# Attention then token mixing on one core: PSUM allocated as one tile of eight banks, and a new order of the steps

## The chip, the core and the metric

The kernel runs on one core of a Trainium2 chip. The core has a matrix engine (PE; its weight loads are listed apart as PEld), a vector engine (DVE), a scalar engine (ACT), a general engine (POOL) and a queue engine (SP) that here issues every DMA. Each engine works through its own instructions in the order in which they were written; engines wait for one another by semaphores only. The metric is device time in microseconds (us) of one execution, as the median of several.

## What is computed

Two layers, one after the other, for 8 batches of 8 heads, 576 positions and 64 columns a head:

```python
q_d = q.reshape(B, H, Sd, 4, D).mean(axis=3)      # the same for k_d, v_d; Sd = 144
out_up = np.repeat(sm_attn(q_d, k_d, v_d), 4, axis=2)      # attention over the pooled positions
scores = np.where(np.abs(pos[:, None] - pos[None, :]) < 4, scale * q @ k.T, -1e9)
out_local = softmax(scores) @ v                            # attention in a band of 7
x = (out_up + out_local)   # [batch, 576, 512], heads side by side

theta = x @ w_theta
y = w_tok_r @ (x * cos(theta)) + w_tok_i @ (x * sin(theta))
u = x + y
out = u + relu(u @ w_ch)
```

## The kernel before

Everything is unrolled. A batch goes through some thirty kinds of step, each written as a Python generator that gives one piece at a time. A string, `ORDER`, has one letter for each piece, 1,240 in all, and says in which order the pieces are recorded; `pin` then chains each engine's instructions in just that order. So the order is written out by hand, and no scheduler moves anything. A second string, `BANKS`, gives the PSUM bank for each piece that needs one.

The steps, with the letters that stand for them and the lines of their main instructions:

- `L` loads q, k and v pieces into one of 15 staging buffers `st` (SP, lines 202 and 205); `C` casts them to bfloat16 (line 218 for v, 221 for q and k; mostly POOL). `l` and `c` do the same for the weights (lines 238 and 240; POOL, 247 and 249).
- `V` and `v`: the token weights are turned on PE (line 261) and copied into `WT` by DVE (line 271), 18 pieces, the first nine for the first half of the output positions.
- `A` and `a`: q and k are turned on PE (286) and copied out by ACT (292). `d`, `e`: sums of four positions (DVE 303; POOL 320 and 321). `U`, `u`, `x`, `P`, `p`, `N`, `n`, `Q`, `q`: the pooled attention (PE 334 to 434; ACT 340, 343, 387; DVE 419, 421, 440).
- `S`, `s`, `m`: banded scores on PE (454), their exponential on ACT (466), the band's mask on DVE (474). `O`, `o`, `i`: the product with v on PE (486) and its normalization on DVE (500, 506). `T`, `t`: the result turned on PE (526) and joined with the pooled one into `xT` by DVE (538).
- `H`, `h`: theta on PE (553), and its cosine and sine by ACT (560 and 561). `G`, `g`, `Z`, `z`: the same for the last 64 positions (PE 571; ACT 578 and 579; DVE 589), with a transposing DMA on SP's queue (595). `X`, `y`: x turned on PE (605) and multiplied with cosine and sine by DVE (610) into `z`.
- `J`, `j`: the token mixing, 64 pieces of nine matmuls each (PE 630, the largest share of PE's work), and the sum `uT` with x on DVE (639). `R`, `f`, `F`: transposing DMAs for the residual (646, 657) and a small POOL copy (652).
- `K`, `b`, `E`, `r`: the channel matmul on PE (665, 671), and ReLU with the residual on DVE (678) into `osb`. `D`, `Y`: stores (691, 697).

PSUM has eight banks of 512 float32 columns. Before the change it is four tiles of two banks each, `pair0` to `pair3`:

```python
pairs = [psum.tile([P, 2, 512], FP32, name=f"pair{i}") for i in range(4)]
```

A step that needs one bank takes it with `one()`, a slice of a pair; a step that needs two takes a whole pair with `two()`. The semaphore waits are not written in the kernel: the recording layer derives them from which instruction touches which part of which tile, and it puts a wait wherever two engines touch the same place of a PSUM tile, reads against reads too.

Of the kernel before, what the change touches and what calls it, by code (L numbers as in the profile page):

```python
# [8 lines left out]
FP32 = mybir.dt.float32  # L9
# [5 lines left out]
P = 128  # L15
# [28 lines left out]
def kernel(  # L44
# [14 lines left out]
    psum = ctx.enter_context(tc.tile_pool(name="psum", bufs=1, space=bass.MemoryType.PSUM))  # L59
# [1 line left out]


    ORDER = (
        "LLkLkCCACLaCLLLALkCCLllaCLLCkLeAkaAkLLadSLeLLkSdsklkklkCcSLkmlPLCcLCCLssOmmCPUlpOCuoiLpCoLlCCOluxxAl"
        "iNncNnaCcCCcnoliTALdaAOnCaLAociLQOaqeLStdoTeTtPsltlimPCcHHplXTCLtpcchVOLHcCCoCXvVilvLlhVvXhTVtCLcyUH"
        "ucvOuyoyVGhvVixvVLxNVlnvgcSNnvSTsnVnLvVvCsZcccAVLLvzVVvVvVCXvTLvyQVValvLqmvCCtAtJaLCLVCOjLJjlmCvLoHO"
        "iOoLlJoheLTLCiJLCLAcjTLtaCiAtdCHTXCCXaLtLHCHALdheyhaChJcCyXGjJUgjyCjCSRuPZupXzCxlJyjAsLcxaLJRmCLJjLf"
        "SsOPRJLjoipCSsjCOoLANNiJCnJnmLOLCnmnaORJjcjoTRoQeLKiCTjUuLiOqtCtTCKtXbJbCHLuoiTxHACXLRjCTtLhHCaXyCtH"
        "eKhdGLhdhbJLLgJSyyjCPPsLjXLpZRyKmKxLRzpbOSsSbJoiCNsmmLNLnAJnnCALnDLCCKLLCJaCCjaObjjOQoTJDCoiKiJqTtUb"
        "ujOjDfLDuOJTCLoiDtLJdLjRoHhjAaLJtKLjiALTHbTaXtChCHCRFtGyCCdCDDRhXECeRrHLXghxeCKSysZzPXyCbyKADLaCJCpx"  # L70
        "JSmjObsoPKJjLmDipjOLoRiOoJiNjnbAaNKnnnLSsDOJACQCoLiTdRJDajqAYCCeCabTtJLTmLjOUutDLJtdoijHfLThHtTLhAjX"
        "tHaGyXKyRguHChhZXKRXSbSdyzfexbLKyJAbJssmmLOPDCCaPFjJopiCOpCjLSoCxjLOismeJNoJRjUiCOnonijDJuDNjAJnCnja"
        "TTQRAuLqLRTttTJXaOxHthtAjoiKXTLtbaHHyhHGhXELDgKdyrShZKyXRKePbbCsyzbSPCmpCxCpJNAsnNJanOSjnnComJODCijj"
        "soOQqofiJTALCYimALTaJTtCRttHaOjoOLJCXhiTJoXRijCTHyetXejhCHtGUdDhjdJgHKyuuRZyXhSjbPzyPJxsppJmSOjoiJjs"
        "JOmjOoSjoixsRiJNKTjmDnNRDnnJfnObOKooQiTJDbqtDFRKTtjHTiXtKtTjHthyHHhGEXJgbZKXhXhzbryyyjRKRJjJjJDbJJJY"
        "RDjJJjjKfKbDjjKRjbfDRRbKDbbDKbFKDDEbrDDY"
    )
    BANKS = (
        "0246024602456024624046304326432016471634562356023140624106207645076452042650645203467301746310274063"
        "6230462046204526014523064132450612543205620476204634062401640132674502645706746017623764502764704261"  # L80
        "4620462064126742567042375460753467401265405260426056452036054360725604275401402370654260520642056023"
        "2460142640367214536401376402764072406362405603267324650124152673542676730167325401"
    )


# [6 lines left out]
            made[tag, k % n] = const.tile(shape, dt, name=f"{tag}_{k % n}")  # L92
        return made[tag, k % n]

    pairs = [psum.tile([P, 2, 512], FP32, name=f"pair{i}") for i in range(4)]
    banks = iter(BANKS)

    def one(dt=FP32):
        i = int(next(banks))
        ap = pairs[i // 2][:, i % 2, :]  # L100
        return ap if dt == FP32 else ap.bitcast(dt)

    def two(dt=FP32):
        ap = pairs[int(next(banks)) // 2][:, :, :]
        return ap if dt == FP32 else ap.bitcast(dt)

    copies = dict(v=nc.vector.tensor_copy, a=nc.scalar.copy, p=nc.gpsimd.tensor_copy)
# [71 lines left out]
    def warm_up():  # L179
        while True:  # L180
            ps = one()
            nc.tensor.matmul(out=ps, lhsT=ident, rhs=warm, start=True, stop=True)
            yield
# [70 lines left out]
    def weight_turns():  # L254
        for hf in range(2):
            for j in range(9):
                ps = held["w", hf, j] = one(BF16)
                for ct in range(3):
                    for ri in ((j % 2,) if j < 8 else (0, 1)):
                        lo, n = (0, P) if j < 8 else (HALF * ri, HALF)  # L260
                        nc.tensor.transpose(
                            out=ps[lo:lo + n, OC * ct:OC * ct + OC],
                            in_=w_tm[ri][0:OC, 3 * hf + ct, P * (j // 2):P * (j // 2) + n],
                            identity=ident[0:OC, 0:OC],
                        )
                yield
# [13 lines left out]
    def turns(b):  # L280
        q_tm, k_tm, v_w = inputs[b]
        parts[b] = (rot("qT", [P, 4, S], BF16, 2), kTs[b % 2], rot("qdT", [P, 4, SD], BF16, 2), kds[b % 2])
        for i, what in TURNS:
            ps = held["turn", b, i, what] = two(BF16).rearrange("p k e -> p (k e)")
            for r in range(WR):
                nc.tensor.transpose(out=ps[:, P * r:P * r + P], in_=(k_tm if what == "k" else q_tm)[:, i, r, :, :], identity=ident)  # L286
            yield
# [41 lines left out]
    def pooled_v(b):  # L329
        v_w = inputs[b][2]  # L330
        psa = held["va", b] = one()
        psb = held["vb", b] = one()
        for c in range(4):
            nc.tensor.matmul(out=psa[KP * c:KP * c + KP, :], lhsT=PU[c], rhs=v_w[:, c, :, 0:D], start=True, stop=True)
        for c in range(4):
            nc.tensor.matmul(out=psb[KP * c:KP * c + KP, 0:2 * D], lhsT=PU[4], rhs=v_w[:, 4, c::4, 0:D], start=True, stop=True)
        yield
# [24 lines left out]
    def pooled_scores(b):  # L362
        qT, kT, qdT, kd = parts[b]

        def heads(dst, hh):
            for m in range(2):
                for par in range(2):
                    nc.tensor.matmul(out=dst(par)[64 * m:64 * m + 64], lhsT=kd[64 * par:64 * par + 64, hh, 2 * m:2 * m + 2, :],
                                     rhs=qdT[64 * par:64 * par + 64, hh, :], start=True, stop=True)

        ps = held["Sd", b, 0] = two()
        for hh in range(3):
            heads(lambda par: ps[:, par, SD * hh:SD * hh + SD], hh)
        yield
        ps = held["Sd", b, 1] = two()
        heads(lambda par: ps[:, par, 0:SD], 3)
        for h in range(H):
            r = KP * (h % 4)
            blk, par = slot(h)
            nc.tensor.matmul(out=ps[r:r + KP, h // 4, SD:2 * SD], lhsT=kd[64 * par:64 * par + 64, blk, 4, :],  # L380
                             rhs=qdT[64 * par:64 * par + 64, blk, :], start=True, stop=True)
        yield
# [390 lines left out]
```

## Time and profile before

| | |
|---|---|
| median of 3 runs | 323.38 us (323.06 to 327.02) |
| the profiled execution | 324.98 us |
| its span, first to last instruction | 323.3 us |
| mean granted clock of PE | 0.939 |
| instructions in the profile | 8,176 |
| bytes moved by DMA | 49.85 MB |

The profile names an instruction by line, engine, operation and tiles (`uT<-pair,xT`: `uT` is written, `pair` and `xT` are read). Behind the busy time of a group stands the idle time of its engine just ahead of the group's instructions, with the releasers, that is, the instructions of other engines whose end let the engine go on. A row of the waits reads: engine and line, what it waited for, the total in us, how often, and the longest. PE's clock is given as the share of full speed that was granted.

### The profile page before, as it was taken

Reading aid. Unit: us, or ns where it says so; the run is one execution under the profiler, and the core shown is the slowest. Engines: PE = TensorE matmul, PEld = TensorE weight load, DVE = VectorE, ACT = ScalarE, POOL = GpSimd, SP = SyncE. Lnnn points to the kernel's source line nnn. Section 1 sums busy time; section 2 is a strip of 40 time slices with the busy share of each in tenths; the row PEclk is TensorE's granted clock in tenths of the full one; section 3 lists DMA queues with packets and bytes.
Section 4 is the critical chain, followed back from the end, with each engine's and each line's share of the span. In section 5 each row is a group of like instructions: output and inputs, shape, how many; then the busy total and the mean of one; then the engine's idle time right before and its main releaser. Section 6 shows DMA issues by size and latency. Waiting matters only on the chain. (4 is left out here: it accounts for less than half of the span.)

```text
span 323.3 us, 8176 instructions
## 1 busy us (share of the span) xinstructions
PE 239.8 (74%) x3344; PEld 162.8 (50%) x3372; DVE 192.4 (60%) x390; ACT 137.4 (43%) x188; POOL 119.5 (37%) x215
## 2 busy tenths in 40 slices
PE   1656975759588897887689587878987888757853
PEld 1535554536356554654357445664665456434510
DVE  2775668637147778672659646667684957624251
ACT  4743656133464195215563277254925650430000
POOL 7667957442329196430704034327032100000000
PEclk9999999598699999997999989999999999997977
DMA  7999996597049998999158838471433032213263
GB/s 234 270 281 237 222 291 168 125 295 217 1 58 193 261 211 218 289 254 152 51 180 133 242 59 163 120 188 47 80 89 83 16 69 81 67 33 96 85 210 98
DMA packets 83173, 49.85 MB, mean 154 GB/s; under 512 B 68160, under 2 KB 68160, under 8 KB 83136
## 3 DMA queue, kind: packets, MB, share of 16 engines
q1 hardware_dynamic: 83136, 49.33, 61.6%
q8 instruction: 26, 0.43, 0.6%
q14 instruction: 11, 0.09, 0.1%
HBM read 34.11 MB, written 9.44 MB: 135 GB/s over the span
## 5 line engine op out<-in xcount | busy, mean ns | idle before, releaser
L630 PE MATMUL pair<-WT,z 128*128 128x288 bf16 x576 | 85.6, 300 | 13.6 <-ACT cs L561 6.1
L630 PEld LDWEIGHTS <-z 128*128 128x128 bf16 x576 | 56.9, 102 | 33.0 <-issue 14.9
L639 DVE TENSOR_TENSOR uT<-pair,xT 128x288 bf16<-128x288 f32 x64 | 28.1, 450 | 46.5 <-PE pair L630 24.6
L665 PE MATMUL pair<-wch,uT 128*128 128x512 bf16 x113 | 34.0, 410 | 11.9 <-DVE osb L678 6.7
L553 PE MATMUL pair<-wth,xT 128*128 128x512 bf16 x116 | 33.0, 404 | 12.5 <-DVE uT L639 4.5
L678 DVE SCALAR_TENSOR_TENSOR osb<-pair,ur 128x512 f32<-128x512 f32 x32 | 21.6, 685 | 24.9 <-ACT cs L561 6.4
L538 DVE TENSOR_TENSOR xT<-pair,xdT 128x464 bf16<-128x464 f32 (+1 forms) x40 | 24.5, 632 | 17.5 <-PE pair L526 5.7
L218 POOL CAST v_w<-st 128x512 bf16<-128x512 f32 x40 | 24.8, 639 | 21.1 <-DMA st<-in_v_dram 20.6
L560 ACT ACTIVATE cs<-pair,pihc 128x512 bf16<-128x512 f32 x32 | 22.1, 692 | 21.8 <-PE pair L553 8.0
L320 POOL TENSOR_TENSOR two<-qT 128x576 f32<-128x576 bf16 x14 | 16.1, 1147 | 40.7 <-ACT qT L292 40.6
L292 ACT COPY qT<-pair 128x1152 bf16<-128x1152 bf16 x16 | 17.9, 1120 | 23.3 <-PE pair L286 23.3
L652 POOL COPY ut<-uT 128x256 bf16<-128x256 bf16 x8 | 3.7, 458 | 65.4 <-DVE uT L639 62.8
L506 DVE TENSOR_TENSOR tmp<-pair,rl 128x512 bf16<-128x512 f32 x40 | 27.1, 684 | 0.7
L610 DVE TENSOR_TENSOR z<-pair,cs 128x1024 bf16<-128x1024 bf16 x32 | 21.6, 682 | 9.3 <-ACT cs L561 3.8
L292 ACT COPY kT<-pair 128x1152 bf16<-128x1152 bf16 x16 | 17.9, 1122 | 18.4 <-PE pair L286 18.4
L466 ACT ACTIVATE pm<-pair 128x1024 bf16<-128x1024 f32 (+1 forms) x24 | 20.6, 882 | 11.4 <-PE pair L454 11.3
L553 PEld LDWEIGHTS <-xT 128*128 128x128 bf16 x128 | 12.1, 102 | 24.7 <-issue 13.5
L665 PEld LDWEIGHTS <-uT 128*128 128x128 bf16 x128 | 12.5, 102 | 24.0 <-issue 14.9
L560 ACT ACT_TABLE_LOAD x8 | 10.3, 1283 | 32.9 <-PE pair L605 14.1
L221 POOL CAST k_tm<-st 128x576 bf16<-128x576 f32 x28 | 19.1, 693 | 13.3 <-DMA st<-in_k_dram 12.9
L349 POOL TENSOR_TENSOR vd<-last,own 128x256 bf16<-128x256 bf16 x16 | 9.8, 622 | 36.9 <-ACT last L343 36.9
L303 DVE TENSOR_REDUCE kd<-kT 128x290 bf16<-128x1160 bf16 x16 | 21.6, 1356 | 0.0
(77 smaller groups left out, 385.8 us busy)
## 6 DMA issues: line engine op xcount, KB each, us to landing
st<-in_v_dram SPq DMA_DIRECT2D x80, 128.0 KB, 3.9
st<-in_k_dram SPq DMA_DIRECT2D x32, 288.0 KB, 4.7
st<-in_q_dram SPq DMA_DIRECT2D x32, 288.0 KB, 5.2
out_dram<-osb SPq DMA_DIRECT2D x32, 256.0 KB, 2.4
st<-in_moe_w_tok_r_dram SPq DMA_DIRECT2D x6, 216.0 KB, 5.7
st<-in_moe_w_tok_i_dram SPq DMA_DIRECT2D x6, 216.0 KB, 6.0
st<-in_moe_w_theta_dram SPq DMA_DIRECT2D x4, 256.0 KB, 5.8
st<-in_moe_w_ch_dram SPq DMA_DIRECT2D x4, 256.0 KB, 4.6
```

The source lines that it names most:

```text
L218: copies[e](out=v_w[:, c, :, 0:D], in_=staged.pop((b, it))[:, 0:DM].rearrange("p (h d) -> p h d", d=D))
L292: copies[e](out=To[:, 2 * i:2 * i + 2, 0:S].rearrange("p a (w r) -> p a w r", r=WR), in_=held.pop(("turn", b, i, what))[:, 0:P * WR].rearr ...
L303: nc.vector.tensor_reduce(out=kd[:, hs, :, 0:PG].rearrange("p e g m -> p (e g) m"), axis=AX.X, op=ALU.add, in_=kT[:, hs, :].rearrange("p e ...
L506: nc.vector.tensor_tensor(out=tmp.rearrange("p g (j d) -> p g j d", d=D), in0=held.pop(("loc", b, c))[:, :, :, 0:D], in1=rls.pop((b, c)).u ...
L538: nc.vector.tensor_tensor(out=xT[:, :, CH * c:CH * c + cnt].rearrange("p e (m j) -> p e m j", j=4), in0=held.pop(("xT", b, c))[:, :, 0:cnt ...
L553: nc.tensor.matmul(out=th, lhsT=xT[:, dc, P * c:P * c + P], rhs=wth[:, dc, :], start=(dc == 0), stop=(dc == 3))
L560: nc.scalar.activation(out=cs[:, 0, :], in_=th, func=AF.Sin, bias=pihc, scale=1.0)
L610: nc.vector.tensor_tensor(out=z_of(b)[:, 2 * c:2 * c + 2, :], in0=held.pop(("xt", b, c)).unsqueeze(1).to_broadcast([P, 2, DM]), in1=css.po ...
L630: nc.tensor.matmul(out=ps, lhsT=z[:, j, P * dc:P * dc + P], rhs=WT[:, j, 288 * hf:288 * hf + 288], start=(j == 0), stop=(j == 8))
L639: nc.vector.tensor_tensor(out=uT[:, dc, cols], in0=held.pop(("u", b, dc, hf)), in1=xT[:, dc, cols], op=ALU.add)
L665: nc.tensor.matmul(out=ps, lhsT=uT[:, dc, P * c:P * c + P], rhs=wch[:, dc, :], start=(dc == 0), stop=(dc == 3))
L678: nc.vector.scalar_tensor_tensor(out=osb, in0=ps, scalar=0.0, in1=rest, op0=ALU.max, op1=ALU.add)
```

## The change

Two edits. PSUM becomes one tile of eight banks, `space`, of which `one()` and `two()` give the same slices as before; and `ORDER` and `BANKS` are replaced by other strings of the same length. Each letter occurs as often as before, so every instruction of the computation is there as before, with the same operands and sizes, in another order and in part in other banks. Lines from 96 on move down by one.

```diff
     ORDER = (
-        "LLkLkCCACLaCLLLALkCCLllaCLLCkLeAkaAkLLadSLeLLkSdsklkklkCcSLkmlPLCcLCCLssOmmCPUlpOCuoiLpCoLlCCOluxxAl"
-        "iNncNnaCcCCcnoliTALdaAOnCaLAociLQOaqeLStdoTeTtPsltlimPCcHHplXTCLtpcchVOLHcCCoCXvVilvLlhVvXhTVtCLcyUH"
-        "ucvOuyoyVGhvVixvVLxNVlnvgcSNnvSTsnVnLvVvCsZcccAVLLvzVVvVvVCXvTLvyQVValvLqmvCCtAtJaLCLVCOjLJjlmCvLoHO"
...
-        "RDjJJjjKfKbDjjKRjbfDRRbKDbbDKbFKDDEbrDDY"
+        "LCkkLCLLCkkLCkLALkLkkALCLLaakCAlaCLkLCLkACdlaSCCSSkcCsLLCeeLdmUussmuOmOLCLoPpPoxiCOoOCipxAaLCCLLAcio"
+        "LliCNCCaAeAnadlTNTnOlaCLdnnoCiSecQTqcLCctLPtllCtspTtCPXHTphmHtUOHuolciluOlcXLLcLGxLhyVycxvhHXNoicygL"
+        "LNnLnnCVLlSVhvVsnVSvvvZszClQCmlCVAqTVAvVLtaClCCvVOvAToaaOviTtlComAaXictHTOcyScloecstcHLiLhhJLXXTVLdc"
+        "HtGvCymJVLVCvLvHgXhZLLyVCCVJlCVvVevyvCVhvVjjvUuClvuJLLSjOOLjsJzJoiAjLLoCCXiJdxaAmJCaSCLjysCOPjLLjpPm"
...
+        "fJRDjDRDbDjbRDKKjjKbbRKbKKbfDbFDDbEDrDDY"
     )
     BANKS = (
-        "0246024602456024624046304326432016471634562356023140624106207645076452042650645203467301746310274063"
+        "0246024670246046204624306462450301546340671026042136012456012406120456210523673465135672561325026452"
...
-    pairs = [psum.tile([P, 2, 512], FP32, name=f"pair{i}") for i in range(4)]
+    space = psum.tile([P, 8, 512], FP32, name="space")
     banks = iter(BANKS)
 
     def one(dt=FP32):
         i = int(next(banks))
-        ap = pairs[i // 2][:, i % 2, :]
+        ap = space[:, i, :]
         return ap if dt == FP32 else ap.bitcast(dt)
 
     def two(dt=FP32):
-        ap = pairs[int(next(banks)) // 2][:, :, :]
+        i = int(next(banks)) // 2
+        ap = space[:, 2 * i:2 * i + 2, :]
         return ap if dt == FP32 else ap.bitcast(dt)
```

More of the change, by code (lines that the diff above doesn't have):

```diff
@@ L63 @@
     ORDER = (
-        "LLkLkCCACLaCLLLALkCCLllaCLLCkLeAkaAkLLadSLeLLkSdsklkklkCcSLkmlPLCcLCCLssOmmCPUlpOCuoiLpCoLlCCOluxxAl"
-        "iNncNnaCcCCcnoliTALdaAOnCaLAociLQOaqeLStdoTeTtPsltlimPCcHHplXTCLtpcchVOLHcCCoCXvVilvLlhVvXhTVtCLcyUH"
-        "ucvOuyoyVGhvVixvVLxNVlnvgcSNnvSTsnVnLvVvCsZcccAVLLvzVVvVvVCXvTLvyQVValvLqmvCCtAtJaLCLVCOjLJjlmCvLoHO"
-        "iOoLlJoheLTLCiJLCLAcjTLtaCiAtdCHTXCCXaLtLHCHALdheyhaChJcCyXGjJUgjyCjCSRuPZupXzCxlJyjAsLcxaLJRmCLJjLf"
-        "SsOPRJLjoipCSsjCOoLANNiJCnJnmLOLCnmnaORJjcjoTRoQeLKiCTjUuLiOqtCtTCKtXbJbCHLuoiTxHACXLRjCTtLhHCaXyCtH"
@@ L69 @@
[L69 to L73, printed above, removed]
@@ L74 @@
-        "soOQqofiJTALCYimALTaJTtCRttHaOjoOLJCXhiTJoXRijCTHyetXejhCHtGUdDhjdJgHKyuuRZyXhSjbPzyPJxsppJmSOjoiJjs"
-        "JOmjOoSjoixsRiJNKTjmDnNRDnnJfnObOKooQiTJDbqtDFRKTtjHTiXtKtTjHthyHHhGEXJgbZKXhXhzbryyyjRKRJjJjJDbJJJY"
-        "RDjJJjjKfKbDjjKRjbfDRRbKDbbDKbFKDDEbrDDY"
+        "LCkkLCLLCkkLCkLALkLkkALCLLaakCAlaCLkLCLkACdlaSCCSSkcCsLLCeeLdmUussmuOmOLCLoPpPoxiCOoOCipxAaLCCLLAcio"
+        "LliCNCCaAeAnadlTNTnOlaCLdnnoCiSecQTqcLCctLPtllCtspTtCPXHTphmHtUOHuolciluOlcXLLcLGxLhyVycxvhHXNoicygL"
@@ new lines @@
+        "LNnLnnCVLlSVhvVsnVSvvvZszClQCmlCVAqTVAvVLtaClCCvVOvAToaaOviTtlComAaXictHTOcyScloecstcHLiLhhJLXXTVLdc"
+        "HtGvCymJVLVCvLvHgXhZLLyVCCVJlCVvVevyvCVhvVjjvUuClvuJLLSjOOLjsJzJoiAjLLoCCXiJdxaAmJCaSCLjysCOPjLLjpPm"
+        "xCpLcolJTiNAjCNnRCJnRRaACOnnoLQjlJiaqjtCcTTJOSCtjLtoURXJfijTHXstmuTHXtuedxHhJLcGLRLHyLhLdhgChJyLyCjc"
+        "RjOoCeiSSJsjZsmKOCPpoLLmCPLbKiAbpxNNLCfnAnnnaXKaKQObyOTqCCzLLCDLLoitTtCJCLoijCCJHThTCJjteAaLLbjUOoCJ"
+        "juALtiRuLCJLXaRdXCdHTxhtDAJjHahyLCHyCGCLCLhLFLCeKCjPPXCDCgXKbRLpJyKZbpjySSCxUEsbNsJmrSunnDOumCLzsAaK"
@@ new lines @@
+        "AjJLoRLbijNnmOoOaTfJnRoiATRQLjiJCCqTOaDOYtKtooCXeLiCHitLTAbhRHtKCTjDaDtCxXyhXLCdHxGHJbeLJhgdyjJjyLhS"
+        "jPPJppdDRKAsjLLZKLzRNXbCLamSbyCSnsnmJDNJjOnsnOOCjooJiQmAioCJejCTRaqfUOijRtOooiLTCKiuTuTttbLDJHHKhjAD"
+        "xaLXLCAdFDbKyXtTLCJLhHCyLeXatGbChjHDJgxJCLjhSSyPDjXyCsmCJLjKsSOpPRZpoizmErRCsAaNJNbnCKnjOnOnooOLioJA"
+        "eDaimRQiJTTjqtATtJaSOjTbJjHtoitsHhjTeXYHKdCCftGXJHbyhdmgjDhyXKhbLCKRbDSOZUuuoyJisRzXjPyPpJjmJOpxoSOj"
+        "JiRDRKoxsNjNimnJnTJbnRjnTJjQjqfOOottKKEbTiDtXoHThFKRirtHTHbtGhJygjZXXHJzyjJhhXDRKyyJYbJjJjRjjJjJJDKJ"
@@ L77 @@
+        "fJRDjDRDbDjbRDKKjjKbbRKbKKbfDbFDDbEDrDDY"
     )
     BANKS = (
-        "0246024602456024624046304326432016471634562356023140624106207645076452042650645203467301746310274063"
-        "6230462046204526014523064132450612543205620476204634062401640132674502645706746017623764502764704261"
-        "4620462064126742567042375460753467401265405260426056452036054360725604275401402370654260520642056023"
-        "2460142640367214536401376402764072406362405603267324650124152673542676730167325401"
+        "0246024670246046204624306450462301546340671026042136012456012406120456210523673465135672561325026452"
@@ L83 @@
+        "4061246023640264012674032764563401523460254602502640123641036731046720467012431267403267340267430462"
+        "0364201645152604236502316725406241021462072640276401764201764572034236017362340623240630640526042670"
+        "1246027564750123672450634542654026542056723740376234520167453745410450670324567103"
     )
```

## The prediction

> **What bounds the kernel now.** I read the page first, then the PE rows of the groups by line, the waits, the busy time by stretches of 20 us, and the timeline at the places where PE stands still.
>
> ```profile
> span 323.3 us, 8176 instructions
> PE 239.8 (74%) x3344; PEld 162.8 (50%) x3372; DVE 192.4 (60%) x390; ACT 137.4 (43%) x188; POOL 119.5 (37%) x215
> ```
>
> No engine is full. PE has the most work, 239.8 us, and stands still for 323.3 - 239.8 = 83.5 us; DVE, the next, has 192.4. DMA is busy too early on, but its bytes are not the limit over the whole span. So the time is PE's work plus PE's waits, and the question is for whom PE waits:
>
> ```profile
> L630 PE MATMUL pair<-WT,z 128*128 128x288 bf16 x576 | 85.6, 300 | 13.6 <-ACT cs L561 6.1 <-DVE uT L639 2.2 <-DVE xT L538 1.4
> L665 PE MATMUL pair<-wch,uT 128*128 128x512 bf16 x113 | 34.0, 410 | 11.9 <-DVE osb L678 6.7 <-DVE z L610 3.4 <-DVE uT L639 0.5
> L553 PE MATMUL pair<-wth,xT 128*128 128x512 bf16 x116 | 33.0, 404 | 12.5 <-DVE uT L639 4.5 <-DVE osb L678 1.9 <-DVE xT L538 1.7
> L526 PE MATMUL pair<-ident,tmp 128*128 128x116 bf16 (+1 forms) x160 | 15.9, 229 | 5.6 <-ACT cs L561 3.6 <-DVE xT L538 0.9 <-DVE uT L639 0.6
> L605 PE MATMUL pair<-ident,xT 128*128 128x128 bf16 x128 | 12.9, 227 | 7.2 <-DVE WT L271 3.4 <-ACT cs L561 2.9 <-DVE xT L538 0.3
> L486 PE MATMUL pair<-v_w,pm 64*64 64x65 bf16 x640 | 12.4, 204 | 2.8 <-DVE tmp L506 1.9 <-DVE xd L421 0.5 <-DVE pm L474 0.3
> L368 PE MATMUL pair<-qdT,kd 64*64 64x144 bf16 x128 | 5.4, 250 | 5.6 <-DVE kd L303 3.6 <-DVE uT L639 1.6 <-POOL qdT L321 0.3
> ```
>
> Behind the second bar stand PE's idle time and who ended it. The mixing matmul of line 630 reads `WT` and `z`, yet it waits for ACT's `cs` and DVE's `uT` and `xT`. It reads nothing that these write, so what it waits for is a place in PSUM that they had to read out first. Taken so, the releasers that give no input are 6.1 + 2.2 + 1.4 = 9.7 at line 630, 6.7 + 3.4 = 10.1 at 665, 4.5 + 1.9 = 6.4 at 553, 3.6 + 0.9 + 0.6 = 5.1 at 526, 2.9 at 605, 1.9 + 0.5 = 2.4 at 486 and 1.6 at 368: 38.2 us, nearly half of the 83.5. These rows don't say whether it is the bank that the matmul is about to write or the other bank of the same pair. Some waits do:
>
> ```profile
> DVE osb L678 <- ACT cs L561: 6.4, 3, 3.7
> DVE uT L639 <- PE pair L605: 4.3, 1, 4.3
> DVE xT L538 <- PE pair L605: 3.5, 3, 1.8
> ```
>
> `osb` is computed from a bank that PE filled and from `ur`; `cs` is read by ACT out of a bank that it does not share. `uT` adds a bank of line 630, and waits for turned x of line 605, which goes into another bank. There is neither data nor a bank between them, only the pair tile. That is the false wait, and it stands on all three engines.
>
> **The tile.** I set the waits of the built kernel beside those of its own order written over one tile of eight banks: on PE 99, on DVE 113 and on ACT 58 instructions then need only an earlier instruction of another engine than before, and no bank is shared that was not shared. The Trainium skill, PSUM — Partial Sum Buffer, section "PSUM bank collisions raise a hardware error", says that engines collide in the same bank and quadrant alone, and tells to guard by bank; by that rule a wait for the neighbour bank protects nothing. No run here shows a collision.
>
> For the price I took PE's 81 stops of over 0.15 us one by one (70.9 us together) and moved each back to the end of the latest wait that the one tile leaves. 23.5 us fall on the neighbour bank directly, of the 38.2. In another 11.8 us PE waits for its own bank, but the DVE or ACT instruction that empties it had itself waited for a neighbour bank. The two largest direct ones:
>
> ```profile
> 84.49 2.32 PE L630 MATMUL pair<-WT,z 128*128 128x288 bf16 x9 [3.96 <-ACT cs L561]
> 311.56 1.29 DVE L678 SCALAR_TENSOR_TENSOR osb<-pair,ur 128x512 f32<-128x512 f32 x2 [2.02 <-DMA ur<-uT]
> 312.90 3.57 PE L665 MATMUL pair<-wch,uT 128*128 128x512 bf16 x8 [3.61 <-DVE osb L678]
> ```
>
> At 312.90 the last channel matmuls stand still for 3.61 us because the other bank of their pair is waiting for `osb`, which waits for the transposing DMA of `ur`. They need neither. At 84.49, 3.15 of 3.96 us are of this kind. So direct and indirect together are 35.3 us; the bounds of what they give back are 0 (something else is due at the same moment each time) and 35.3. What is late next is seen here:
>
> ```profile
> 289.03 0.49 ACT cs L561
> ...
> 290.16 0.68 DVE osb L678
> 290.84 1.79 DVE z L610 x3
> 292.63 0.38 DVE uT L639
> 293.05 1.85 PE pair L630 x9
> ```
>
> These are pieces of the chain of waits, and the timeline has DVE's idle time ahead of them:
>
> ```profile
> 289.55 0.69 DVE L678 SCALAR_TENSOR_TENSOR osb<-pair,ur 128x512 f32<-128x512 f32 x1 [3.72 <-ACT cs L561]
> ```
>
> `osb` waits for `cs` without need, and behind it on DVE's queue stand three products `z` and a `uT`, then the mixing of line 630. Without the wait `osb` would have run inside DVE's idle 3.7 us and the products would start up to 0.7 to 1.3 us sooner; but `z` needs that same `cs`, so of 3.72 us of idle time only about a third comes back. At the end of the span, on the other hand, nothing else is due and nearly all of 3.6 comes back. Between a third and all I take two thirds: 0.67 x 35.3 = 23.5 us.
>
> **The clock.** PE's clock falls after its stops:
>
> ```profile
> 60.00:80.00 20.00, 14.92 (x146) 9.58 (x147) 10.28 (x21) 5.72 (x6) 8.20 (x12) 0.78 0.89 249
> 80.00:100.00 20.00, 13.74 (x225) 9.84 (x223) 6.96 (x15) 12.09 (x18) 8.85 (x16) 0.83 0.32 56
> 100.00:120.00 20.00, 17.90 (x236) 12.36 (x238) 15.59 (x31) 8.76 (x14) 12.24 (x18) 1.00 1.05 217
> 300.00:320.00 20.00, 13.18 (x61) 6.18 (x59) 7.24 (x14) 0.00 (x0) 0.40 (x1) 0.83 0.42 134
> ```
>
> The columns are the stretch, busy PE, PEld, DVE, ACT and POOL, then the granted clock. It is 1.00 where PE is busy for 17.9 of 20 us, and 0.78 to 0.83 where it is busy for 13 to 15. In the three slow stretches 20 x (0.22 + 0.17 + 0.17) = 11.2 us of full clock are missing. PE is busy for two thirds of that, about 7.5 us, and of the stops that cause it two of the largest are those above; I take 3 us back, with bounds of 0 and 7.5. The Trainium skill, TensorE: Matmul & The Clock Gate, Part 1, says the clock is half or full, and halves after about 3.4 us of idleness. By that only the stops of 3.4 us and more count, and the gain would be nearer 2; the sum goes by the rows.
>
> **The new order.** Counts and sizes stay, so PE's 239.8 us stay. In the old order the twelve pieces of the token weights all go out on SP's queue ahead of the first transposing DMA `z`; in the new one five of them stand behind it, and 36 instead of 33 loads go out up to the tenth weight piece.
>
> ```profile
> st<-in_k_dram SPq DMA_DIRECT2D x32, 288.0 KB, 4.7
> out_dram<-osb SPq DMA_DIRECT2D x32, 256.0 KB, 2.4
> st<-in_moe_w_tok_i_dram SPq DMA_DIRECT2D x6, 216.0 KB, 6.0
> L247 POOL CAST uT<-st 96x576 bf16<-96x576 f32 x12 | 8.3, 703 | 3.0 <-DMA st<-in_moe_w_tok_i_dram 1.8 <-DMA st<-in_moe_w_tok_r_dram 1.2
> L271 DVE COPY WT<-pair 128x288 bf16<-128x288 bf16 x18 | 4.9, 295 | 1.8 <-PE pair L261 0.9 <-PE pair L553 0.9
> 40.00:60.00 20.00, 13.74 (x244) 10.77 (x244) 15.03 (x33) 9.90 (x16) 11.46 (x19) 0.88 0.75 201
> 47.66 1.43 SPq L202 DMA_DIRECT2D st<-in_v_dram  x2
> 56.95 1.31 SPq L595 DMA_TRANSPOSE z<-zT  x1
> 57.19 0.59 PE L605 MATMUL pair<-ident,xT 128*128 128x128 bf16 x4 [3.43 <-DVE WT L271]
> 61.25 2.32 PE L630 MATMUL pair<-WT,z 128*128 128x288 bf16 x9 [1.17 <-DVE xT L538]
> 72.90 2.36 PE L630 MATMUL pair<-WT,z 128*128 128x288 bf16 x9
> ```
>
> Three loads of 288 KB at 201 to 249 GB/s (the last column of the stretches) are 3.5 to 4.3 us later for the first half of the weights. At 47.66 + 1.43 SP's queue stands for 7.9 us before the transposition at 56.95, as `zT` isn't there yet; whatever is behind it waits too, and now that is five weight pieces and then `v` loads. Who waits for them: POOL's casts, PE's line 261, DVE's copies to `WT`, and the second half of the mixing of batch 0. The new order, however, puts the turns of the second half among the first mixings instead of ahead of them, so the 3.43 us that PE lost at 57.19 behind that row of copies may go. Bounds: 3.4 gained, 4.3 lost; I take 2 lost, as the loads are certain and the gain depends on the order of eleven other things. In the later batches the attention steps of the next batch stand some 20 places earlier and stores some 58 later. SP has nothing else to do at the end, and it puts loads ahead of stores, so I cost that at nothing; if a late store holds one of the five `osb` buffers, DVE waits for it, up to 2.4 us a time (the median landing). The end is the same in kind: six channel matmuls, their ReLU and stores behind the last mixing.
>
> **The sum.** 323.3 - 23.5 - 3 + 2 = 298.8 us of span. The profiled execution took 324.98, 1.7 over its span, and the median of the runs, 323.38, is 1.6 under it, so the median is about the span: 299 us.
>
> **The rivals.** *The next wait takes over.* The stops on a neighbour bank go, but their own bank, the data or the next place on DVE's queue is nearly as late, as in the rows at 289 to 293. A quarter comes back: 323.4 - 9 = 314. For it: DVE is busy for 60% and its queue is strict; against it: the two stops of 3.15 and 3.6 us alone are 6.8. *Nothing is seen.* The new order spends what the tile gives, or the false waits lay beside true ones throughout: 323, give or take 6. Against it speaks the end of the span, where nothing covers. *Slower.* `z` is late once more, at 57, with five weight pieces behind it: landing takes 6.0 us, five casts of 0.70 are 3.5 and nine copies of 0.30 are 2.7, so the weights are whole at about 57 + 12.2 = 69 instead of 57. If the first mixing waits for that, 10 to 15 us are lost, and the loads of the next batches behind it move too, so that the tile's gain goes into waiting for DMA: about 334. It decides from the point at which `zT` comes after 55 us; against it: the fourth mixing group before began only at 72.9. *Better than forecast.* All of 35.3, 4 of clock and the 3.4 at 57 come back: 323.4 - 42.7 = 281.
>
> **How the numbers follow.** The forecast has 0.60, the rivals 0.17, 0.09, 0.06 and 0.08 in the order named. A measurement tells 2% from no change, 6.5 us; faster by more means under 316.9. The forecast and the last rival lie there, and three quarters of the first: 0.60 + 0.08 + 0.13 = 0.81. Within 2%: 0.04 + 0.09 = 0.13; slower 0.06. The forecast's own range is 290 to 307 (0.9 and 0.5 of 35.3, and the bounds of clock and order). From 284 to 318 it takes in the first rival too, and leaves out the slow one, most of the one in which nothing is seen and half of the best.
>
> **What would show it.** In the waits of the changed kernel `osb` should no longer be released by `cs`, nor `uT` by line 605, and PE's idle time should fall from 83.5 to about 60 with 239.8 of work falling by a few. The stop of 3.6 us ahead of the last channel matmuls should be gone, and the clock of the last stretch be nearer 1. The order is wrong if SP's queue stands longer before its first transposition and PE stops for `WT` between 55 and 90 us. The forecast is wrong on the tile if PE's idle time stays near 83 with its own banks named as releasers, and on its size if the rows at the end give back 3.6 us and those in the middle nothing.

## The result, and the profile after

The changed kernel takes 244.96 us (median of 4 runs, 244.22 to 246.41) against 323.22 for the kernel before: a ratio of 0.7595, with a 95% interval of 0.7542 to 0.7648. That is 78 us less where 24 were forecast, and well under the range.

First the page of the changed kernel, its head and the PE rows of the groups by line (columns as before; `space` is now what `pair` was, and every line number is one higher):

```profile
span 242.7 us, 8203 instructions
PE 215.5 (89%) x3372; PEld 152.6 (63%) x3372; DVE 188.8 (78%) x390; ACT 136.6 (56%) x188; POOL 122.3 (50%) x215
...
PEclk9999979999999999999999999999999999999998
...
L631 PE MATMUL space<-WT,z 128*128 128x288 bf16 x576 | 79.4, 286 | 1.4 <-DMA z<-zT 1.4
L554 PE MATMUL space<-wth,xT 128*128 128x512 bf16 x128 | 33.7, 391 | 0.2 <-ACT kT L293 0.2
L666 PE MATMUL space<-wch,uT 128*128 128x512 bf16 x128 | 31.6, 379 | 0.0
...
L606 PE MATMUL space<-ident,xT 128*128 128x128 bf16 x128 | 11.8, 222 | 0.0
```

PE's idle time is 242.7 - 215.5 = 27.2 us instead of 83.5. The mixing of line 631 waits 1.4 us instead of 13.6, theta's matmul 0.2 instead of 12.5, the channel matmul nothing instead of 11.9. What is left in these rows is mostly a wait for data, for the DMA that brings `z`; the 0.2 us for `kT` are for a place. But the busy time fell too, by 24.3 us, with the same matmuls. The clock row is below 9 in two of forty slices; its first slices stand for a time in which no clock is on record, as told below.

By stretches of 20 us (the stretch, then busy PE, PEld, DVE, ACT and POOL, the granted clock, DMA's share and its GB/s), and the timeline of the end:

```profile
0.00:20.00 20.00, 8.49 (x172) 6.35 (x172) 11.78 (x37) 11.33 (x14) 13.28 (x54) 1.00 0.88 252
...
60.00:80.00 20.00, 19.29 (x375) 15.53 (x375) 15.10 (x34) 10.91 (x14) 15.43 (x24) 1.00 1.02 232
...
180.00:200.00 20.00, 20.00 (x301) 14.07 (x300) 17.57 (x35) 13.12 (x19) 5.01 (x8) 1.00 0.43 99
```

```profile
229.33 2.37 PE L631 MATMUL space<-WT,z 128*128 128x288 bf16 x18
...
231.53 5.34 PE L666 MATMUL space<-wch,uT 128*128 128x512 bf16 x24
...
236.71 1.03 PE L672 MATMUL space<-wch,ut 128*128 128x512 bf16 x4
...
238.99 1.14 SPq L698 DMA_DIRECT2D out_dram<-osb  x2
```

From 60 us on PE is nearly full. In the first 20 us, where it waits for the first loads, it is busy for 8.5; that is the largest part, 11.5 us, of what is left of its idle time. At the end 24 channel matmuls run without a gap; the stop of 3.6 us is gone.

### The profile page after: what moved, and what is told of

Same layout as the page of the kernel before. It is cut to its first block, busy times and chain, and to the rows that moved or that the text cites. A ratio compares the mean times of both kernels' runs of the same rounds, so it can differ in the third digit from the quotient of the medians.

```text
span 242.7 us, 8203 instructions
## 1 busy us (share of the span) xinstructions
PE 215.5 (89%) x3372; PEld 152.6 (63%) x3372; DVE 188.8 (78%) x390; ACT 136.6 (56%) x188; POOL 122.3 (50%) x215
## 4 chain that ended last, share of the span: by engine, by line
PE 64%; DMA 16%; POOL 7%; SPq 4%; issue 3%; DVE 3%; ACT 1%; DVEq 0%; POOLq 0%; ACTq 0%
PE space L631 25%; PE space L554 11%; PE space L666 7%; PE space L287 4%; DMA out_dram<-osb 3%; DMA z<-zT 3%; SPq L203 3%; PE space L606 3%; PE space L527 3%; PE space L487 2%; DMA st<-in_q_dram 2%; DMA st<-in_k_dram 2%; DMA st<-in_moe_w_tok_i_dram 2%; PE space L455 2%; POOL k_tm L222 2%
## 5 line engine op out<-in xcount | busy, mean ns | idle before, releaser
L631 PE MATMUL space<-WT,z 128*128 128x288 bf16 x576 | 79.4, 286 | 1.4 <-DMA z<-zT 1.4
L640 DVE TENSOR_TENSOR uT<-space,xT 128x288 bf16<-128x288 f32 x64 | 28.7, 451 | 16.4 <-PE space L631 15.9
L219 POOL CAST v_w<-st 128x512 bf16<-128x512 f32 x40 | 25.4, 638 | 24.3 <-DMA st<-in_v_dram 18.6
L554 PE MATMUL space<-wth,xT 128*128 128x512 bf16 x128 | 33.7, 391 | 0.2 <-ACT kT L293 0.2
L666 PE MATMUL space<-wch,uT 128*128 128x512 bf16 x128 | 31.6, 379 | 0.0
L539 DVE TENSOR_TENSOR xT<-space,xdT 128x464 bf16<-128x464 f32 (+1 forms) x40 | 24.4, 629 | 4.1 <-PE space L527 4.1
L507 DVE TENSOR_TENSOR tmp<-space,rl 128x512 bf16<-128x512 f32 x40 | 27.0, 680 | 0.5
L467 ACT ACTIVATE pm<-space 128x1024 bf16<-128x1024 f32 (+1 forms) x24 | 20.5, 881 | 10.4 <-PE space L455 10.3
L679 DVE SCALAR_TENSOR_TENSOR osb<-space,ur 128x512 f32<-128x512 f32 x32 | 21.6, 685 | 5.9 <-PE space L666 2.9
L561 ACT ACTIVATE cs<-space,pihc 128x512 bf16<-128x512 f32 x32 | 22.2, 695 | 4.4 <-PE space L554 4.1
L561 ACT ACT_TABLE_LOAD x8 | 10.3, 1283 | 25.3 <-PE space L554 20.7
L611 DVE TENSOR_TENSOR z<-space,cs 128x1024 bf16<-128x1024 bf16 x32 | 21.6, 681 | 3.6 <-PE space L606 2.6
L321 POOL TENSOR_TENSOR two<-qT 128x576 f32<-128x576 bf16 x14 | 16.0, 1144 | 13.6 <-ACT qT L293 13.6
```

Of the source, the lines that this page charges most:

```text
L219: copies[e](out=v_w[:, c, :, 0:D], in_=staged.pop((b, it))[:, 0:DM].rearrange("p (h d) -> p h d", d=D))
L507: nc.vector.tensor_tensor(out=tmp.rearrange("p g (j d) -> p g j d", d=D), in0=held.pop(("loc", b, c))[:, :, :, 0:D], in1=rls.pop((b, c)).u ...
L539: nc.vector.tensor_tensor(out=xT[:, :, CH * c:CH * c + cnt].rearrange("p e (m j) -> p e m j", j=4), in0=held.pop(("xT", b, c))[:, :, 0:cnt ...
L554: nc.tensor.matmul(out=th, lhsT=xT[:, dc, P * c:P * c + P], rhs=wth[:, dc, :], start=(dc == 0), stop=(dc == 3))
L561: nc.scalar.activation(out=cs[:, 0, :], in_=th, func=AF.Sin, bias=pihc, scale=1.0)
L611: nc.vector.tensor_tensor(out=z_of(b)[:, 2 * c:2 * c + 2, :], in0=held.pop(("xt", b, c)).unsqueeze(1).to_broadcast([P, 2, DM]), in1=css.po ...
```

## The experiments

The change is two edits, so the first question is which of them did it. The theory: the waits for the neighbour bank, all of them, and not only the 23.5 us that PE meets directly. The rivals: the count was right and the new order gives the rest; or the edits only work together.

**e1, the tile alone.** Old `ORDER` and `BANKS`, new tile; `one()` and `two()` follow as in the change.

```diff
-    pairs = [psum.tile([P, 2, 512], FP32, name=f"pair{i}") for i in range(4)]
+    space = psum.tile([P, 8, 512], FP32, name="space")
```

> The old ORDER and BANKS, with PSUM as one tile of eight banks: the first edit alone. If the false waits carry nearly all of the gain, and the step-by-step count of 35.3 us was short because one false wait delays others through the queues, this takes 250 to 262 us, with PE idle for some 35 us. If the count was right and the new order carries the rest, it takes 285 to 300 us. If the two edits only work together, it stays over 310 us.

Measured: 258.12 us, ratio 0.7918 (0.7825 to 0.8011).

```profile
span 256.4 us, 8211 instructions
PE 221.6 (86%) x3372; PEld 154.6 (60%) x3372; DVE 190.4 (74%) x390; ACT 136.7 (53%) x188; POOL 120.1 (47%) x215
...
L631 PE MATMUL space<-WT,z 128*128 128x288 bf16 x576 | 81.2, 289 | 7.2 <-DMA z<-zT 5.5 <-DVE osb L679 1.0 <-DVE xd L422 0.4
...
L666 PE MATMUL space<-wch,uT 128*128 128x512 bf16 x128 | 31.9, 379 | 1.0 <-ACT cs L562 1.0
```

PE's idle time is 34.8 us. Five sixths of the whole gain come from the one tile, without a change of order; the first theory holds.

**e2, the order alone.** New `ORDER` and `BANKS`, four tiles of two banks.

> The new ORDER and BANKS, with PSUM as four tiles of two banks: the second edit alone. If the false waits are the whole matter, this is as slow as before or slower, 318 to 335 us, since its waits for a neighbour bank are as many as before (99 on PE, 107 on DVE and 74 on ACT against 99, 113 and 58). If the order carries half of the gain by itself, it takes 275 to 295 us.

Measured: 308.39 us, ratio 0.9488 (0.9407 to 0.9569), between the ranges of the two theories.

```profile
span 307.1 us, 8199 instructions
PE 233.4 (76%) x3372; PEld 160.5 (52%) x3372; DVE 189.7 (62%) x390; ACT 137.4 (45%) x188; POOL 118.3 (39%) x215
```

The order is worth 15 us over pairs and 13 over one tile (258.12 to 244.96; 10 if the two ratios are compared). 0.7918 x 0.9488 = 0.751 against the measured 0.7595: the two edits are almost independent.

**e3, larger tiles.** The old order with two tiles of four banks.

```diff
-    space = psum.tile([P, 8, 512], FP32, name="space")
+    spaces = [psum.tile([P, 4, 512], FP32, name=f"space{i}") for i in range(2)]
```

> The old ORDER and BANKS, with PSUM as two tiles of four banks. If any two instructions of different engines on one tile are put in sequence, whatever the bank, a tile of four couples each bank with three others instead of one: against the one tile 265 waits on PE, 258 on DVE and 171 on ACT then differ. By the false-wait theory the time is well over that of before, 370 to 450 us, with PE idle for over 130 us. If tiles only matter by their number of instructions or slices, it is between 245 and 325 us.

Measured: 447.25 us, the middle of two runs, 437.36 and 457.14. The page of the quicker one:

```profile
span 435.7 us, 8227 instructions
PE 275.8 (63%) x3372; PEld 179.3 (41%) x3372; DVE 193.3 (44%) x390; ACT 139.7 (32%) x188; POOL 119.2 (27%) x215
```

Coupling each bank to three others costs 179 us over e1 in the quicker run and 199 in the other, to one other 66. DVE and ACT are as busy as ever; PE alone stands 160 us. That the one tile of eight is free of this is the work of the recording layer: it keeps the banks of a tile that is all of PSUM apart, and those of a tile of two or four banks it doesn't. Why it draws the line there, no run shows.

**e4 to e7, the waits by kind.** Over the one tile and the old order, the pairs' waits are written back as added semaphore waits: all (e4), or one kind. The banks' use stays as in e1. The core of the edit, with notes put in here behind the #:

```diff
+            for other, name in touched.get(p, {}).items():     # p: the pair that ins touches
+                if other == mine:
+                    continue
+                kind = "R" if "PE" not in (mine, other) else ("W" if mine == "PE" else "E")
+                if kind in COUPLE:                              # e4 "WER", e5 "W", e6 "E", e7 "R"
+                    tc.add_manual_dep(ins, name, mybir.DependencyInfo(
+                        mybir.DependencyClass.Sync, mybir.DependencyReason.DATA), reason="pair")
+            touched.setdefault(p, {})[mine] = ins.name
```

> The old order over one tile, with the neighbour-bank waits of the pairs written back by hand as added semaphore waits (control). If these waits are all that the four tiles cost, it is back at 318 to 330 us. If the four tiles cost something else too (addresses, names, slices), it stays well under that, near 258.

> The old order over one tile, with only those neighbour-bank waits written back in which PE waits for DVE or ACT to empty the other bank of the pair. The count of the prediction puts 23.5 us on these: 276 to 286 us, if waits add up. If a wait alone is mostly absorbed and they only hurt together (PE waits for an emptying that itself waits for PE), it takes 258 to 268 us.

> The old order over one tile, with only those neighbour-bank waits written back in which DVE or ACT waits for PE to finish filling the other bank of the pair. The count puts most of the indirect 11.8 us here: 264 to 272 us if waits add up, 258 to 262 if they only hurt together with PE's. If delays go on through the queues further than one step back, it takes 275 us or more.

> The old order over one tile, with only those neighbour-bank waits written back in which DVE waits for ACT or ACT for DVE, both of them reading PSUM. By the count they are the smallest part: 258 to 264 us. If e5, e6 and e7 lie over e1 by about 65 us in all, the waits add up and the count was too small by itself; if by far less, they multiply.

| run | waits written back | us | ratio to before (95%) | over e1, by ratio x 323.2 us |
|---|---|---|---|---|
| e4 | all | 327.85 | 1.011 (0.996 to 1.025) | 70.7 |
| e5 | PE for the emptying of the other bank | 284.57 | 0.873 (0.864 to 0.882) | 26.3 |
| e6 | DVE or ACT for the filling of the other bank | 282.94 | 0.863 (0.852 to 0.874) | 23.0 |
| e7 | DVE for ACT, ACT for DVE | 268.44 | 0.825 (0.815 to 0.835) | 10.8 |

The control e4 is the kernel before again, to within its interval of 1.5%, so these waits are what the four tiles cost. Its page and the waits that the prediction named show the same groups with nearly the same figures:

```profile
span 327.6 us, 8234 instructions
PE 245.6 (75%) x3372; PEld 160.5 (49%) x3372; DVE 192.2 (59%) x390; ACT 137.6 (42%) x188; POOL 119.4 (36%) x215
...
DVE osb L679 <- ACT cs L562: 6.4, 3, 3.7
...
PE space L631 <- ACT cs L562: 6.1, 2, 4.0
```

The kinds come to 60 us one by one and 71 together. They add up, as the one theory of e7 said; the 11 us between are about what the intervals leave open. e5 came out where adding up had it, e6 where delays go on for more than one step, and e7 above its range. The waits on the emptying side, E and R, cost 34 us, no less than the 26 of those in PE's own queue, though DVE and ACT have idle time to spare. The heads of the pages of e5, e6 and e7:

```profile
span 288.0 us, 8254 instructions
PE 233.0 (81%) x3372; PEld 157.4 (55%) x3372; DVE 194.7 (68%) x390; ACT 137.3 (48%) x188; POOL 119.8 (42%) x215
...
span 285.2 us, 8207 instructions
PE 227.9 (80%) x3372; PEld 157.5 (55%) x3372; DVE 188.9 (66%) x390; ACT 137.1 (48%) x188; POOL 119.9 (42%) x215
...
span 264.7 us, 8205 instructions
PE 221.6 (84%) x3372; PEld 153.5 (58%) x3372; DVE 190.3 (72%) x390; ACT 136.5 (52%) x188; POOL 120.4 (45%) x215
```

**e8, the weights ahead of z.** One letter of the changed kernel moves, the first `z`.

```diff
-        "LNnLnnCVLlSVhvVsnVSvvvZszClQCmlCVAqTVAvVLtaClCCvVOvAToaaOviTtlComAaXictHTOcyScloecstcHLiLhhJLXXTVLdc"
+        "LNnLnnCVLlSVhvVsnVSvvvZsClQCmlCVAqTVAvVLtaClCCvVOvAToaaOviTtlComAaXictHTOcySclzoecstcHLiLhhJLXXTVLdc"
```

> The changed kernel with one letter moved: the transposing DMA z of batch 0 goes out on SP's queue behind the twelfth piece of the token weights instead of ahead of the last five. If the prediction's term for the order is right (weights 3.5 to 4.3 us late, 2 us lost), this is 2 to 4 us faster than the changed kernel, 241 to 243 us. If the weights had slack, as there is no stop of PE for WT in the changed kernel's trace, it is the same within 1%, 243 to 248 us.

Measured: 246.93 us, ratio 0.759 (0.7455 to 0.7724), within 1% of the changed kernel, as the second theory had it. The interval alone would leave room for the 2 us of the prediction, and the `z` of batch 0, now later, stops PE for 0.58 us. The trace of the changed kernel says more: its last weight pieces go out at 48.24 us, where before the change the last went out at 45.04, and still PE has no stop of over 0.15 us for `WT`. The weights had slack.

**e9, z right behind zT.** The old order over one tile; each `z` moves to just behind its `Z`.

```diff
-        "ucvOuyoyVGhvVixvVLxNVlnvgcSNnvSTsnVnLvVvCsZcccAVLLvzVVvVvVCXvTLvyQVValvLqmvCCtAtJaLCLVCOjLJjlmCvLoHO"
+        "ucvOuyoyVGhvVixvVLxNVlnvgcSNnvSTsnVnLvVvCsZzcccAVLLvVVvVvVCXvTLvyQVValvLqmvCCtAtJaLCLVCOjLJjlmCvLoHO"
...
-        "eKhdGLhdhbJLLgJSyyjCPPsLjXLpZRyKmKxLRzpbOSsSbJoiCNsmmLNLnAJnnCALnDLCCKLLCJaCCjaObjjOQoTJDCoiKiJqTtUb"
+        "eKhdGLhdhbJLLgJSyyjCPPsLjXLpZzRyKmKxLRpbOSsSbJoiCNsmmLNLnAJnnCALnDLCCKLLCJaCCjaObjjOQoTJDCoiKiJqTtUb"
```

> The old order over one tile, with each batch's transposing DMA z put on SP's queue right behind the step that computes zT, ahead of the residual transpositions and loads that stood between. In e1 PE stops for z for 5.5 us in all, 2.7 of them at 106.5 us, where z was issued 2.7 us after zT was done. If SP's queue is what makes z late, the stops for z fall from 5.5 to under 3 us and the time from 258 to 253 to 256 us, a fifth to a third of what the new order gives. If z is late because its chain starts late (theta of the last 64 positions), the other two stops stay, and the time is 256 to 259 us.

Measured: 272.49 us, ratio 0.8439 (0.8315 to 0.8563): 14 us slower than e1, where the theories had 253 to 259. Waits of e1, then of e9, and behind them the same of SP's queue:

```profile
DVE osb L679 <- DMA ur<-uT: 9.1, 4, 4.2
...
PE space L631 <- DMA z<-zT: 5.5, 3, 2.7
...
SPq L596 <- DVE zT L590: 18.1, 6, 5.9
```

```profile
DVE osb L679 <- DMA ur<-uT: 20.1, 6, 6.3
POOL v_w L219 <- DMA st<-in_v_dram: 18.6, 6, 11.0
...
PE space L455 <- DVE osb L679: 5.9, 2, 3.6
...
PE space L631 <- DMA z<-zT: 1.3, 1, 1.3
...
SPq L596 <- DVE zT L590: 23.0, 7, 5.9
```

The stops for `z` do fall, from 5.5 to 1.3 us. But SP's queue now stands for `zT` for 23.0 us instead of 18.1, with residual transpositions and loads behind it: `osb` waits 20.1 instead of 9.1 us for `ur`, holds DVE, and PE waits for DVE. This is read from the waits; no run took it apart. I had looked at the wait that I removed and not at what was queued behind the instruction that I moved.

**e10, the old distances in the new order.** In the changed kernel those of the two kinds of transposing DMA that stand further ahead of their users than in the old order move later, to the old distance; loads and stores pass them by. One line of eleven as an example:

```diff
-        "xCpLcolJTiNAjCNnRCJnRRaACOnnoLQjlJiaqjtCcTTJOSCtjLtoURXJfijTHXstmuTHXtuedxHhJLcGLRLHyLhLdhgChJyLyCjc"
+        "xCpLcolJTiNAjCNnCJnaACOnnoRLQjlJiaqjtCcTTJOSCtjLtRoUXJfijTHXsRtmuTHXtuedxHhJLcGLLHyLhLdhgChJyLyRCjcj"
```

> The changed kernel with only SP's transposing DMAs moved later: each z and each residual R stands as many letters ahead of its batch's first mixing piece or first ReLU piece as in the old order (z 29, 19, 8, 7, 8, 10, 3, 9 instead of 67, 45, 13, 7, 21, 10, 10, 12; the last R of a batch 30, 8, 20, 3, 4, 15, 6, 2 instead of 74, 46, 32, 25, 18, 15, 18, 2). If these distances are what the new order gives, most of its 13 us are lost again: 252 to 260 us, with DVE's waits for the residual DMA back from 1.0 to 5 us or more. If the gain comes from the order on the computing engines, it stays at 243 to 248 us.

Measured: 248.28 us, ratio 0.7653 (0.757 to 0.7737).

```profile
DVE osb L679 <- DMA ur<-uT: 7.1, 2, 5.5
...
PE space L631 <- DMA z<-zT: 5.0, 3, 2.5
```

The waits come back almost to those of e1 (in the changed kernel they are 1.0 and 1.4), but only 2 to 3 of the order's 10 to 13 us come back, and the intervals overlap. So the distances are a small part. What else in the order is worth some 8 us wasn't taken apart further and stays open. The traces of e1 and the changed kernel say only where it shows: 34.8 - 27.2 = 7.6 us less idle time of PE and 6.1 less busy time.

## Why the prediction was wrong

*What bounds the kernel* was right: PE's waits. Of its 83.5 us of idle time 38.2 stood behind releasers that give no input, 23.5 of these on the neighbour bank, and false waits stood on all three engines. The named groups went nearly as it said: in e1 `osb` is not released by `cs` at all, nor `uT` by the turned x, and the stop ahead of the last matmuls is gone. In the changed kernel `osb` is still released by `cs` once, for 1.3 us; why, the trace doesn't say.

*The sum* took 23.5 us of idle time and 3 of busy time off for the tile. e4 and e1 differ in nothing but the false waits, and between them lie 327.6 - 256.4 = 71.2 us of span: 82.0 - 34.8 = 47.2 of PE's idle time and 245.6 - 221.6 = 24.0 of its busy time. Of the 44.7 us that the sum missed, 11.8 are the third that it took off the count, 11.9 are what the count of 35.3 had not found, and 21.0 are busy time. These are the terms that failed, and with them the one for the order.

*The direct count*, 23.5 us of idle time, was about right: with those waits alone PE stands 55.0 - 34.8 = 20.2 us longer than in e1 (e5, whose profiled execution of 289.7 us was the longest of its five). That e5's time is 26.3 us longer comes near the count in part by chance, as there is busy time in it.

*The indirect count* is the step of the argument that failed. It put 11.8 us on delays of DVE and ACT; in e6 and e7 PE stands 22.5 and 8.3 us longer than in e1, and the time is 34 us longer. It went back one step only, from a stop of PE to the emptying instruction and what that had waited for. A delay on DVE's queue also moves everything behind it, and by way of PE, ACT and the next emptying it can come back later as a wait that looks like one for an own bank or for data. That path is argued: e6 and e7 price it without following it. So "the bounds of what they give back are 0 and 35.3" was no bound.

*The two thirds* failed as well: all of the count came back, and more. The argument from the rows at 289 us, that something else is due anyway, holds for one stop looked at by itself. That with all waits gone what is due next moves forward too is how I read it, not something that a run shows by itself.

*PE's work "falling by a few"*: from the tile alone it fell by the 24.0 us above (the profile of before lacks 28 of the 3,372 matmul records, so I set e4 against e1). One part is the clock. The stretches recorded at half clock of e4, of e1 and of the changed kernel, their sums (the last has only one in which PE works):

```profile
sum 44.40, PE 36.70 PEld 22.12 DVE 15.45 ACT 7.74 POOL 8.87; mean PE 4.59 PEld 2.77 DVE 1.93 ACT 0.97 POOL 1.11
...
sum 17.00, PE 15.46 PEld 10.60 DVE 12.09 ACT 8.13 POOL 14.47; mean PE 5.16 PEld 3.53 DVE 4.03 ACT 2.71 POOL 4.82
...
32.20:35.60 3.40, 3.40 (x22) 1.69 (x15) 2.40 (x4) 3.10 (x5) 2.99 (x5) 0.50 0.84 234
```

PE is busy at half clock for 36.7, 15.5 and 3.4 us. Nine mixing matmuls take 2.36 us in such a stretch (at 72.90 in the kernel before) and 1.26 out of it, so about half of this busy time is extra, and e4 to e1 gains (36.7 - 15.5) / 2 = 10.6 us, e1 to the changed kernel another 6.0. The term of the prediction was 3, with 7.5 as its bound, from three stretches of 20 us; over its whole span the kernel before is busy at half clock for 29.3 us on record. The rule of the Trainium skill that stood beside it (TensorE: Matmul & The Clock Gate, Part 1: the clock halves after some 3.4 us of idleness) would have given less still, and the traces do not agree with it, as the last section shows.

The record of the clock leaves out the start. The profile prints 1.00 up to the first change on record, at 41.9 us in e4 and 24.6 in e1, but the matmuls run at half clock there. The same nine turns of line 287 in e1, before and behind that point:

```profile
21.76 1.12 PE L287 MATMUL space<-ident,k_tm 128*128 128x128 bf16 x9
...
24.88 0.66 PE L287 MATMUL space<-ident,q_tm 128*128 128x128 bf16 x9
```

Up to there PE is busy for 24.1 us in e4, 12.0 in e1 and 12.7 in the changed kernel (to 25.3 us), so up to another 6.0 us of e4 to e1 are the clock's. That is an estimate, as the smallest matmuls are less than twice as long there. The mean granted clocks, 0.939 for the kernel before among them, come out too high for the same reason.

The other 7 us or so go with the number of stops, 73 of over 0.15 us in e4 and 31 in e1. A group of nine mixing matmuls behind a wait, in the chain and in the timeline of before, then one in a stream, in those of the changed kernel:

```profile
295.43 1.28 PE pair L630 x9
...
295.43 1.26 PE L630 MATMUL pair<-WT,z 128*128 128x288 bf16 x9 [0.55 <-DVE uT L639]
```

```profile
65.84 1.10 PE space L631 x9
...
65.68 1.27 PE L631 MATMUL space<-WT,z 128*128 128x288 bf16 x9
```

Both groups are as long, but the one in a stream starts under the end of the matmuls before it, and that part counts once: 1.28 against 1.10 is 0.18 us, and 42 stops fewer make some 8 us of this. No run changed the stops alone, and the profile models the ends of matmuls, so that part is an estimate.

*The order* was given 2 us of loss and brought 10 to 13 of gain. The loss was for weights landing later; they do land later, and had slack (e8). One gain, of at most 3.4 us, was set against it; the others were left at nothing, as they hang on "the order of eleven other things".

*The rivals.* What happened is nearest to the last, "better than forecast", but its 281 was built on the bound of 35.3 and is still 36 us too high. The one with the next wait taking over is refuted by e1.

## What to carry to other kernels

Where a releaser in the profile gives an instruction neither data nor its place, look at what the waits are derived from, here the size of a PSUM tile, and price it on all engines: those on the engines that empty the banks cost no less than those on the bottleneck (34 against 26 us here). A count along the trace, stop by stop, came out at half for a cause that repeats everywhere; to get its size, take it away as a whole, as e1 does, or put it back by kind. And the bottleneck's busy time is no constant: with the false waits 24 us of it went, by the clock and by the overlap of matmul groups.

## What the runs showed that was not expected

PE's clock halves without a long stop. In e1 no stop of PE between its first and its last matmul is over 2.83 us, yet the clock fell three times, and in the first of these stretches PE was busy for 9.02 of the 10.2 us at half clock. The stops around the start of the first stretch and of the last (timeline, then stretches):

```profile
26.42 0.68 PE L287 MATMUL space<-ident,k_tm 128*128 128x128 bf16 x9 [0.88 <-POOL k_tm L222]
...
28.60 1.14 PE L287 MATMUL space<-ident,q_tm 128*128 128x128 bf16 x9 [1.25 <-POOL q_tm L222]
...
106.51 0.42 PE L631 MATMUL space<-WT,z 128*128 128x288 bf16 x1 [2.69 <-DMA z<-zT]
...
28.00:38.20 10.20, 9.02 (x115) 5.79 (x116) 5.46 (x9) 7.01 (x10) 9.94 (x15) 0.50 0.83 210
...
106.50:109.90 3.40, 3.05 (x29) 2.61 (x30) 3.23 (x7) 0.00 (x0) 1.41 (x2) 0.51 1.03 359
```

A stop of 2.69 us ended as the clock fell to half, and at 28.0 us a stop of 1.25 was under way. The lengths at half clock while PE works are multiples of 3.4 us in these traces. The number of stops alone doesn't set the clock: e7 has 44 of over 0.15 us and a mean granted clock of 0.979, e1 has 31 and 0.967.
